# An attention and SwiGLU block on one Trainium2 core: another ScalarE price in the planner, GpSimd work in halves, and a rebuilt end

## The chip, the cores and the metric

The kernel runs on one core of one Trainium2 chip. The core has five engines with instruction queues of their own: TensorE (PE in the profile; its weight loads are PEld), VectorE (DVE), ScalarE (ACT), GpSimd (POOL) and SyncE (SP), which here issues every DMA. They meet through semaphores only. The metric is the device time of one execution in microseconds; lower is better.

## The reference, cut to what matters

One batch of 2048 tokens, model width 512, 32 heads of 16, FFN width 1792, all bf16:

```python
xn  = layernorm(x)
qkv = (xn @ wqkv) -> q, k, v per head          # 32 heads, head size 16
p   = softmax(q @ k.T * 16 ** -0.5)            # 2048 x 2048 per head
att = (p @ v).reshape(2048, 512) @ wo
ffn = (silu(xn @ w1) * (xn @ w3)) @ w2
out = x + att + ffn
```

## The kernel before

**Tiling.** The queries are cut into 4 chunks of 512, the heads into 8 groups of 4; a chunk and a group make a unit, 32 in all. A unit has 64 pairs: one block of 128 keys, two heads of the group, 512 queries. A pair is two score matmuls (L1774) into two neighbouring PSUM banks, then an exponential over 128x1024 elements, then matmuls with V into PSUM bank 7, where a row of ones beside V gathers the softmax's denominator (L2027). There are 2048 score matmuls, so 1024 pairs.

**Two ways to exponentiate.** A pair goes to ScalarE as one activation (L1837, tile PT), or to VectorE as integer arithmetic on bf16 bit patterns: L1909 ("p1") reads the scores from PSUM, and a chain of four instructions over two such pairs, L1951, L1958, L1967 and L1973, makes three bf16 arrays in tile xd whose products with V are summed. So a VectorE pair costs three times the V matmuls of a ScalarE pair. Three PSUM buffers of two banks (0-1, 2-3, 4-5) hold scores; bank 6 takes all dense tiles: projections, FFN, output.

**End of a unit.** VectorE copies bank 7 into U (L2045); DMAs bring the denominators into Lc; VectorE takes reciprocals (L2065); DMAs spread them over the partitions as R. For every second unit GpSimd multiplies U by R into onorm (L2092, 128x512, 15 times; function `e5`). Unit 30's half is multiplied on VectorE (L2086), and unit 31, the last, has a path of its own (`last_end`): ScalarE copies bank 7 (L2107), small fp32 matmuls sum and spread (L2114, L2132), VectorE multiplies (L2140).

**Output tiles.** `tile_OUT(tg, part)` makes 128 tokens of output. Part 3 sums the 14 FFN groups in PSUM, and VectorE adds the residual xr and keeps the result as fp32 in osum (L1599). Part 4 (first three chunks) and part 2 (last chunk) sum the attention groups; VectorE adds osum (L1612) and a DMA of 128 KB stores the tile (L1619). Part 2 of every second tile adds osum in PSUM instead, through an fp32 identity matmul (L1593, tile idf), and ScalarE may copy it out (L1608). A group is four matmuls of 32 output columns each that run side by side.

**Order.** A planner, `_Sched`, writes out the whole order of every engine's queue when the kernel is built. It steps a clock of its own by 0.02 us and hands out work as engines come free, with prices for each instruction (`a_cost` ScalarE, `d_cost` VectorE from PSUM, `s_cost` VectorE from SBUF), a tail until others see a result (`_TAILS`), and gaps between matmuls of one tiling and the other (`_time`). VectorE takes a pair whenever it is about to come free (`try_d`, `d_due`); ScalarE takes the others (`try_a`). On the chip the queues run in that order, each as its semaphores allow. `bg` lists the FFN and output tiles in the order wanted; `dense_banks` and `start_tile` let them in. `left[u]` counts a unit's pairs not yet scored, `st["pos"]` the score matmuls issued. In the last unit VectorE gets no pairs when `left` is at `D_STOP` = 6.

**The very end.** Every engine loads a flag and branches around a slow path that this data doesn't need; then SyncE waits on all 24 DMA semaphores (`emit_end`, L141).

Of the kernel before, what the change touches and what calls it, by code (L numbers as in the profile page):

```python
# [13 lines left out]
_NDMA_SEMS = 24  # L14
# [6 lines left out]
class _Prog:  # L21
# [115 lines left out]
    def emit_end(self, e, handle, dma_sems):  # L137
        if e == "sp":
            for i in range(_NDMA_SEMS):
                if self.dma_final[i] > 0:  # L140
                    handle.wait_ge(dma_sems[i], self.dma_final[i])  # L141


_LAT = 0.06
_LATS = {("pe", "act"): 0.041, ("pe", "dve"): 0.053, ("dve", "pool"): 0.083, ("pool", "dve"): 0.033, ("act", "dve"): 0.033}
_TAILS = {"act": 0.182, "dve": 0.083, "pool": 0.05, "sp": 0.0}


class _Sched(_Prog):
# [25 lines left out]
    def _time(self, op, deps, dur, tail, mode=None, rows=None):  # L175
# [7 lines left out]
        if mode == "row":  # L183
            if lm == "row":
                gap = 0.217 if rows & lr else 0.007
            else:
                gap = 0.318
            start = max(ready, ls + gap)
            self.pem = (mode, rows | lr if gap < 0.1 and start < ls + 0.2 else rows, start)
            self.free["pe"] = start + 0.01  # L190
        elif mode == "col":
            start = max(ready, ls + (0.217 if lm == "col" else 0.318))
            self.pem = (mode, frozenset(), start)
            self.free["pe"] = start + 0.2
        else:
            start = max(ready, ls + (0.217 if lm == "x" else 0.318))
            self.pem = (mode, frozenset(), start + dur - 0.217)
            self.free["pe"] = start + dur
# [838 lines left out]
def _plan_fast(nc, ps, flag, A_x, A_wqkv, A_wo, B_w1, B_w3, B_w2, out):  # L1037
# [30 lines left out]
    NW = 3  # L1068
    PVQ = 28
    A_SOON = 0.7  # L1070
    D_SOON = 0.6
# [15 lines left out]
    with ctx:  # L1087
# [67 lines left out]

        a_cost = lambda n: 0.049 + 0.000834 * n
        d_cost = lambda n: 0.054 + 0.00106 * n
# [364 lines left out]
        def tiles_FFN(sc, fc):  # L1522
# [40 lines left out]
            def cond_g():  # L1563
# [4 lines left out]
                if sc > 0 and not all(("HF", (sc - 1) * 4 + i) in done for i in range(4)):  # L1568
# [3 lines left out]
                    _T("Y%d_%d" % (sc, fc), mk(1), evac_u, cond=lambda: ("G%d_%d" % (sc, fc)) in done)]  # L1572

        ON_B = (NQC * NP) % NON

        def tile_OUT(tg, part):
            qc, ts = divmod(tg, 4)

            def og(g, slot, key):
                return (lambda i: onorm[:, slot, ts * 128 + 32 * i:ts * 128 + 32 * i + 32], wo[:, g, :],  # L1580
                        [("ON", slot), ("wor", g)],
                        lambda: have(key))
            ffn = [(lambda i, fc=fc: hT[:, fc, ts * 128 + 32 * i:ts * 128 + 32 * i + 32], w2[:, fc, :],
                    [("hT", fc), ("w2", fc)], None) for fc in range(FC)]
            ats = [og(g, (qc * NP + g) % NON, ("ON", qc, g)) for g in range(NP)]
            gr = {2: ats + [og(NP - 1, ON_B, ("ON", qc, "B"))], 3: ffn, 4: ats, 0: ffn + ats}[part]
            by_pe = part == 2 and ts % 2 == 1
            groups = []
            for k, (lh, rh, rd, cd) in enumerate(gr):
                groups.append((lambda e, bk, lh=lh, rh=rh, k=k: col_groups(lh, rh, D)(  # L1590
                    e, bk, k == 0, k == len(gr) - 1), rd, cd, DG))
            if by_pe:
                groups.insert(1, (lambda e, bk: e.matmul(bank(bk), idf[:, :], osum[:, ts, :], start=False, stop=False),  # L1593
                                  [("idf",), ("osum", ts)], None, 0.95))

            def evac(bk, o, rel):
                def e1(eng="dve"):
                    if part == 3:
# [6 lines left out]
                        return  # L1605
                    other = osum[:, ts, :] if part in (2, 4) else xr[:, ts % 2, :]
                    if by_pe and eng == "act":
                        fn = lambda e: e.activation(osb[:, ts, :], bank(bk), ACTF.Identity)  # L1608
                    elif by_pe:
                        fn = lambda e: e.tensor_copy(osb[:, ts, :], bank(bk))  # L1610
                    else:
                        fn = lambda e: e.tensor_tensor(osb[:, ts, :], bank(bk), other, ALU.add)  # L1612
                    q = P.op(eng, fn,
                             reads=[("ps", bk), ("osum", ts) if part in (2, 4) else ("xr", ts % 2)],
                             writes=[("osb", ts), ("xn", ts)],
                             dur=d_cost(512) if eng == "dve" else a_cost(512))
                    rel(q)
                    done[("XE", tg)] = q.end
                    P.post("sp", lambda: P.dma(lambda e: e.dma_start(out_v[:, tg, :], osb[:, ts, :]),  # L1619
                                               reads=[("osb", ts)], writes=[("out", tg)], kb=128),  # L1620
                           ready=q.end + _LAT, prio=1)
                if by_pe:
                    P.post2({"dve": lambda: e1("dve"), "act": lambda: e1("act")}, ready=o.end + _LAT,
                            prios={"dve": 2, "act": 1})
                else:
                    P.post("dve", e1, ready=o.end + _LAT, prio=1, cond=lambda: part in (2, 4) or ("xr", tg) in done)

            def cond():
                if part == 4:
                    return have(("OSUM", tg), ("ON", qc, NP - 1))  # L1630
                if part == 2:
                    return have(("OSUM", tg)) and st["pos"] >= NR
                if not have(*[("hT", qc, fc) for fc in range(FC)]):
# [7 lines left out]
            def start():  # L1641
                def load():
                    P.dma(lambda e: e.dma_start(xr[:, ts % 2, :], x_v[:, tg, :]), writes=[("xr", ts % 2)], kb=128)
                    done[("xr", tg)] = P.t
                P.post("sp", load, ready=P.t, prio=1, cond=lambda: tg < 2 or ("XE", tg - 2) in done)
            return _T("O%d_%d" % (tg, part), groups, evac, cond=cond, start=None if part in (2, 4) else start)


        st = {"dbl": 0, "pos": 0, "pv": 0, "dbal": 0, "nd": 0, "lastA": -1.0, "n_exp": 0, "wait_a": 0, "hold_d": 0, "last_par": 0}
        pbuf = [0.0] * 3  # L1650
# [40 lines left out]
        for sc in range(NQC):  # L1691
# [5 lines left out]
            for ts in range(4):  # L1697
                bg.append(tile_OUT(sc * 4 + ts, 3))
        for ts in range(4):
            bg.append(tile_OUT((NQC - 1) * 4 + ts, 2))  # L1700
# [8 lines left out]
        def dense_banks():  # L1709
            if st["pos"] >= NR and st["n_exp"] >= NR:  # L1710
                return [6, 0, 1, 2, 3, 4]
            if st["pos"] == 0:
                return [6, 4, 5, 2, 3]
            if st["early"]:
                return [6, 4, 5]
            return [6]
# [158 lines left out]
        def try_d():  # L1875
# [28 lines left out]
            def p1():  # L1904
                if sl["y"] is None:
                    sl["y"] = free_slot(yfree)
                    yfree[sl["y"]] = 1e9
                ys = sl["y"]
                q = P.op("dve", lambda e: e.tensor_scalar(dsl[:, ys, 1024 * c:1024 * c + 1024], ps[:, b0 * 512:b0 * 512 + 1024],  # L1909
                                                          YB, G_LO, ALU.add, ALU.max),  # L1910
# [128 lines left out]
        def unit_end(u, o):  # L2039
# [33 lines left out]
            def e4():  # L2073
# [4 lines left out]
                if h or u == NU - 2:  # L2078
                    eng = "dve" if u == NU - 2 else "pool"
                    P.post(eng, lambda: e5(eng), ready=q.end + _LAT, prio=0, cond=lambda: u // 2 < NON or all(  # L2080
                        ("OUT", (u // 2 - NON) // NP * 4 + i) in done for i in range(4)))

            def e5(eng):
                on = (u // 2) % NON
                if u == NU - 2:
                    q = P.op(eng, lambda e: e.scalar_tensor_tensor(onorm[:, on, :], U[:, 0, :], msk[:, 0:1], R[:, :],  # L2086
                                                                   ALU.mult, ALU.mult),
                             reads=[("Uc",), ("msk", 0)] + [("R", j_, h_) for j_ in range(4) for h_ in range(2)],
                             writes=[("ON", on)], dur=0.68)
                    done[("ON", qc, pi)] = q.end + _LAT  # L2090
                    return
                q = P.op(eng, lambda e: e.tensor_tensor(onorm[:, on, :], U[:, 0, :], R[:, :], ALU.mult),  # L2092
                         reads=[("Uc",)] + [("Uo", j_) for j_ in range(4)] +
                         [("R", j_, h_) for j_ in range(4) for h_ in range(2)], writes=[("ON", on)],
                         dur=0.6 if eng == "dve" else 1.3)
                done[("ON", qc, pi)] = q.end + _LAT
                done[("e5", u // 2)] = q.end
            if u == NU - 1:
# [3 lines left out]
        def last_end(o):  # L2102
# [36 lines left out]
            def norm_b():  # L2139
                q = P.op("dve", lambda e: e.scalar_tensor_tensor(onorm[:, ON_B, :], U[:, 1, :], msk[:, 1:2], bank(PV),  # L2140
                                                                 ALU.mult, ALU.mult),
                         reads=[("Ut",), ("ps", PV), ("msk", 1)], writes=[("ON", ON_B)], dur=0.597)
                done[("ON", qc, "B")] = q.end + _LAT
# [5 lines left out]
        def start_tile(urgent_only):  # L2149
            banks = [b for b in dense_banks() if bank_free[b] <= P.t and not any(a.bank == b for a in active)]  # L2150
            if not banks or len(active) >= (4 if st["pos"] >= NR or st["pos"] == 0 else 2):
                return
# [30 lines left out]
        def try_dense():  # L2183
            start_tile(False)
            for a in active:
# [6 lines left out]
                if not a.groups:  # L2192
# [5 lines left out]
                    if a.name[0] == "O":  # L2198
                        tg_, pt_ = a.name[1:].split("_")
                        if pt_ != "3":  # L2200
                            done[("OUT", int(tg_))] = o.end
                        if pt_ in "013":
                            done[("HF", int(tg_))] = o.end
# [147 lines left out]
```

## Time and profile before

| | |
|---|---|
| median of 8 runs | 801.57 us (800.11 to 803.56) |
| the profiled execution | 800.48 us, span 798.7 us, mean granted TensorE clock 0.997 |
| busy in the span | PE 754.2, DVE 766.1, ACT 774.9, POOL 33.1 us |
| exponentials on ScalarE (L1837) | 801, 1160 ns each on average |
| pairs on VectorE (L1909) | 223, 1216 ns each |
| VectorE chain L1951, L1958, L1967, L1973 | 112 each; 697, 1232, 681, 709 ns |
| GpSimd multiplications (L2092) | 15, 1508 ns each |
| fp32 identity matmuls (L1593) | 4 instructions, 2.3 us in all |

The span runs from the first to the last instruction; the time has some 2 us around it. In the profile a line such as `L1837 ACT ACTIVATE f_PT<-ps ... x801 | 751.9, 1160 | 4.8 <-PE` gives line, engine, operation, output and inputs, count, busy time in us, mean ns of one, and the engine's idle time before them with what ended it. Instructions of one engine overlap at their ends, so the mean of one is longer than the distance between two. In a timeline a row gives start and length in us, engine, line and count, and in brackets the idle time before it and who ended that.

### The profile page before, as it was taken

How to read it: one execution, taken by the hardware profiler on the slowest of the kernel's cores; microseconds unless marked ns; L12 is line 12 of the kernel's file. 1: busy time of each engine (PE TensorE's matmuls, PEld its weight loads, DVE VectorE, ACT ScalarE, POOL GpSimd, SP SyncE). 2: the span in 40 equal slices, each digit the busy share in tenths (PEclk: the TensorE clock that was granted, in tenths of full speed). 3: DMA queues.
4: the chain of work that ended last, by engine and by line, in shares of the span. 5: the costliest groups of instructions: out<-in, count | busy, mean ns of one | idle time of the engine just before them, and what ended most of it. 6: DMA issues, size and time to landing. Idle time of an engine off the chain costs nothing.

```text
span 798.7 us, 21147 instructions
## 1 busy us (share of the span) xinstructions
PE 754.2 (94%) x9157; PEld 222.6 (28%) x9157; DVE 766.1 (96%) x1032; ACT 774.9 (97%) x876; POOL 33.1 (4%) x45
## 2 busy tenths in 40 slices
PE   8998999999999999999999999999999999999996
PEld 6322322222222222222222222222222222222222
DVE  8898999999999999999999999999999999999984
ACT  6999999999999999999999999999999999999993
POOL 3100100000000000000000000000000000000000
PEclk9999999999999999999999999999999999999998
DMA  7032233332222233133221233322123341232211
GB/s 212 2 62 67 16 42 35 43 46 23 48 37 29 29 46 49 32 46 55 36 21 31 33 48 44 53 28 51 20 22 41 48 55 19 51 34 23 29 8 33
DMA packets 83727, 32.91 MB, mean 41 GB/s; under 512 B 72104, under 2 KB 80040, under 8 KB 83624
## 3 DMA queue, kind: packets, MB, share of 16 engines
q1 hardware_dynamic: 83624, 31.46, 27.4%
q8 instruction: 74, 1.21, 0.6%
q14 instruction: 29, 0.24, 0.1%
HBM read 22.81 MB, written 2.10 MB: 31 GB/s over the span
## 4 chain that ended last, share of the span: by engine, by line
ACT 65%; DVE 18%; PE 14%; issue 1%; DMA 1%; POOL 0%; SPq 0%; DVEq 0%
ACT f_PT L1837 62%; DVE f_xd L1909 5%; PE ps L1328 5%; PE ps L1774 5%; PE ps L2027 4%; DVE f_xd L1958 3%; ACT f_th L1542 3%; DVE f_xd L1951 2%; DVE f_xd L1973 1%; DVE f_xd L1967 1%; DVE f_t L1546 1%; DVE f_hT L1556 1%; DVE f_stats L1252 1%; DMA f_R<-f_Rrow 1%; DVE f_U L2045 0%
## 5 line engine op out<-in xcount | busy, mean ns | idle before, releaser
L1837 ACT ACTIVATE f_PT<-ps 128x1024 bf16<-128x1024 f32 x801 | 751.9, 1160 | 4.8 <-PE ps L1774 2.6
L1774 PE MATMUL ps<-f_QT,f_KT 32*128 32x512 bf16 x2048 | 313.7, 385 | 25.9 <-ACT f_PT L1837 17.5
L1909 DVE TENSOR_SCALAR f_xd<-ps 128x1024 int16<-128x1024 f32 x223 | 271.1, 1216 | 4.9 <-PE ps L1774 3.7
L2027 PE MATMUL ps<-f_PT,f_Vaug 128*17 128x512 bf16 (+1 forms) x1602 | 211.7, 385 | 1.0 <-DVE f_U L2045 0.4
L2027 PE MATMUL ps<-f_xd,f_Vaug 128*17 128x512 bf16 (+1 forms) x1338 | 185.9, 385 | 4.3 <-DVE f_U L2045 1.8
L1774 PEld LDWEIGHTS ps<-f_QT,f_KT 32*128 32x128 bf16 x2048 | 79.1, 91 | 332.6 <-ACT f_PT L1837 272.2
L1328 PE MATMUL ps<-f_xnT,f_w 128*32 128x512 bf16 x1792 | 140.7, 384 | 3.9 <-DVE f_t L1546 3.2
L1958 DVE TENSOR_TENSOR f_xd<-f_xd 128x2048 bf16<-128x2048 bf16 x112 | 138.0, 1232 | 0.0
L1951 DVE TENSOR_SCALAR f_xd<-f_xd 128x2048 int16<-128x2048 int16 x112 | 78.0, 697 | 2.2 <-PE ps L2027 1.6
L1973 DVE TENSOR_SCALAR f_xd<-f_xd 128x2048 int16<-128x2048 int16 x112 | 79.4, 709 | 0.0
L1967 DVE TENSOR_SCALAR f_xd<-f_xd 128x2048 int16<-128x2048 int16 x112 | 76.3, 681 | 0.0
L1328 PE MATMUL ps<-f_w,f_hT 128*32 128x512 bf16 x896 | 75.5, 384 | 0.0
L2027 PEld LDWEIGHTS ps<-f_PT,f_Vaug 128*17 128x17 bf16 (+1 forms) x1602 | 50.9, 92 | 58.6 <-issue 45.7
L2027 PEld LDWEIGHTS ps<-f_xd,f_Vaug 128*17 128x17 bf16 (+1 forms) x1338 | 44.8, 92 | 49.9 <-issue 27.3
L1328 PEld LDWEIGHTS ps<-f_xnT,f_w 128*32 128x32 bf16 x1792 | 36.1, 94 | 62.5 <-issue 52.4
L2092 POOL TENSOR_TENSOR f_onorm<-f_U,f_R 128x512 bf16<-128x512 f32 x15 | 22.6, 1508 | 709.8 <-DMA f_R<-f_Rrow 709.8
L1542 ACT ACTIVATE f_th<-ps 128x512 f32<-128x512 f32 x56 | 41.6, 743 | 0.0
L1546 DVE SCALAR_TENSOR_TENSOR f_t<-f_th,ps 128x512 bf16<-128x512 f32 x56 | 38.0, 679 | 1.8 <-ACT f_th L1542 1.3
L1556 DVE SCALAR_TENSOR_TENSOR f_hT<-f_t,ps 128x512 bf16<-128x512 bf16 x56 | 38.0, 678 | 0.8 <-PE ps L1328 0.6
L1328 PEld LDWEIGHTS ps<-f_w,f_hT 128*32 128x32 bf16 x896 | 17.9, 94 | 25.5 <-issue 21.3
L1328 PE MATMUL ps<-f_wo,f_onorm 128*32 128x512 bf16 x272 | 21.5, 384 | 0.8 <-DVE f_wkv L1599 0.3
L2045 DVE COPY f_U<-ps 128x512 f32<-128x512 f32 x31 | 21.2, 684 | 0.0
(82 smaller groups left out, 239.2 us busy)
## 6 DMA issues: line engine op xcount, KB each, us to landing
f_w<-in_B_w_dram SPq DMA_DIRECT2D x112, 128.0 KB, 2.4
f_R<-f_Rrow SPq DMA_DIRECT2D x124, 32.0 KB, 4.0
f_xr<-in_A_x_dram SPq DMA_DIRECT2D x16, 128.0 KB
out_dram<-f_xn_sb SPq DMA_DIRECT2D x16, 128.0 KB
f_U<-f_U SPq DMA_DIRECT2D x60, 32.0 KB, 2.0
f_w<-in_B_w_dram SPq DMA_DIRECT2D x7, 256.0 KB
f_xd<-in_A_x_dram SPq DMA_DIRECT2D x3, 512.0 KB
f_xd<-in_A_x_dram SPq DMA_DIRECT2D x2, 256.0 KB
```

The costliest lines, as they stand in the source:

```text
L1328: ins = e.matmul(bank(bk)[32 * i:32 * i + 32, 0:ncols], make_lhsT(i), rhs_ap, start=start, stop=stop, tile_position=(0, 32 * i))
L1542: q = P.op("act", lambda e: e.activation(th[:, ss, :], bank(bk), ACTF.Tanh, scale=0.5), reads=[("ps", bk)], writes=[("th", ss)], dur=a_cos ...
L1546: q2 = P.op("dve", lambda e: e.scalar_tensor_tensor(t1[:, ss, :], th[:, ss, :], 1.0, bank(bk), ALU.add, ALU.mult), reads=[("th", ss), ("ps ...
L1556: q = P.op("dve", lambda e: e.scalar_tensor_tensor(hT[:, fc, :], t1[:, ss, :], 0.5, bank(bk), ALU.mult, ALU.mult), reads=[("t1", ss), ("ps ...
L1774: ins = e.matmul(bank(b), l_, r_, start=True, stop=True, tile_position=(rp, 0))
L1837: q = P.op("act", lambda e: e.activation(PT[:, s_, :], ps[:, b0 * 512:(b0 + 2) * 512], ACTF.Exp, scale=ASC, bias=ABIAS), reads=[("ps", b0) ...
L1909: q = P.op("dve", lambda e: e.tensor_scalar(dsl[:, ys, 1024 * c:1024 * c + 1024], ps[:, b0 * 512:b0 * 512 + 1024], YB, G_LO, ALU.add, ALU. ...
L1951: P.op("dve", lambda e: e.tensor_scalar(dsl[:, NY + m_, 0:n], y, 0x7F, 0x3F00, ALU.bitwise_and, ALU.bitwise_or), reads=YK, writes=[("ds", ...
L1958: q_ = P.op("dve", lambda e: e.tensor_tensor(t_ap.bitcast(BF16), y.bitcast(BF16), t_ap.bitcast(BF16), ALU.mult), reads=YK + [("ds", NY + m ...
L1967: q_ = P.op("dve", lambda e: e.tensor_scalar(g_ap, y, -G_LO, 0.0, ALU.add, ALU.max), reads=YK, writes=[("g", g_, k) for k in range(n // 51 ...
L1973: q_ = P.op("dve", lambda e: e.tensor_scalar(y, y, 0x7F80, None, ALU.bitwise_and), reads=YK, writes=YK, dur=s_cost(n), name="e", lock=True)
L2027: ins = e.matmul(bank(PV)[32 * j:32 * j + (17 if g % 2 == 0 else 32), :], v_, p_, start=s0, stop=s1, tile_position=(0, 32 * j))
```

## The change

- The planner's price of a ScalarE instruction goes from 0.049 + 0.000834 n to 0.0615 + 0.000834 n us, its tail from 0.182 to 0.105; three gaps between matmuls change by 0.002 to 0.007.
- The GpSimd multiplication is cut into two of 128x256 (`e5h`). Each is issued in the planner step in which an L1909 is issued, and waits on the VectorE instruction before that L1909. Output tiles read onorm by halves.
- L2086 is posted 2.5 us later in the planner's clock (`R_LAG`).
- The fp32 identity matmuls go. The last chunk's first three tiles take part 3 and part 2 with VectorE's addition; its fourth tile is one sum in PSUM (part 5): 14 FFN groups, the residual through a bf16 identity, the attention groups; ScalarE copies it out.
- `late()`: output tiles of the last chunk may start, and bank 4 may be used for them, when the last unit has at most 6 pairs to be scored, VectorE holds none and buffer 2 is free; before, this came when all scores were issued. The fourth tile waits for `late()`.
- The last chunk's outputs are stored by two DMAs of two tiles each.
- At the end SyncE waits only on the DMAs that it doesn't know to be done from waits before.

```diff
-            for i in range(_NDMA_SEMS):
-                if self.dma_final[i] > 0:
-                    handle.wait_ge(dma_sems[i], self.dma_final[i])
+            left = [op for op in self.ops["sp"] if op.token[1] == self.dma_final[op.token[0][1]]
+                    and self.known.get(op.token[0], 0) < op.token[1]]
+            for op in left:
+                handle.wait_ge(dma_sems[op.token[0][1]], op.token[1])
...
-_TAILS = {"act": 0.182, "dve": 0.083, "pool": 0.05, "sp": 0.0}
+_TAILS = {"act": 0.105, "dve": 0.083, "pool": 0.05, "sp": 0.0}
...
-                gap = 0.318
+                gap = 0.325
...
-            start = max(ready, ls + (0.217 if lm == "col" else 0.318))
+            start = max(ready, ls + (0.219 if lm == "col" else 0.32))
...
+    R_LAG = 2.5
...
-        a_cost = lambda n: 0.049 + 0.000834 * n
+        a_cost = lambda n: 0.0615 + 0.000834 * n
...
+        def late():
+            return left[NU - 1] <= D_STOP and st["hold_d"] == 0 and pbuf[2] <= P.t or st["pos"] >= NR
...
-            gr = {2: ats + [og(NP - 1, ON_B, ("ON", qc, "B"))], 3: ffn, 4: ats, 0: ffn + ats}[part]
-            by_pe = part == 2 and ts % 2 == 1
+            last_b = [og(NP - 1, ON_B, ("ON", qc, "B"))]
+            res = [(lambda i: ident[:, 32 * i:32 * i + 32], xr[:, ts % 2, :], [("ident",), ("xr", ts % 2)],
+                    lambda: have(("xl", tg)))]
+            gr = {2: ats + last_b, 3: ffn, 4: ats, 5: ffn + res + ats + last_b}[part]
...
-            if by_pe:
-                groups.insert(1, (lambda e, bk: e.matmul(bank(bk), idf[:, :], osum[:, ts, :], start=False, stop=False),
-                                  [("idf",), ("osum", ts)], None, 0.95))
...
+                    if part == 5:
+                        q = P.op("act", lambda e: e.activation(osb[:, ts, :], bank(bk), ACTF.Identity),
+                                 reads=[("ps", bk)], writes=[("osb", ts), ("xn", ts)], dur=a_cost(512))
...
+                    fin_o.append(ts)
+                    if len(fin_o) % 2 == 0:
+                        t0, t1 = sorted(fin_o[-2:])
+                        P.post("sp", lambda: P.dma(lambda e: e.dma_start(
+                            out_v[:, 4 * qc + t0:4 * qc + t1 + 1:t1 - t0, :], osb[:, t0:t1 + 1:t1 - t0, :]),
...
-                    return have(("OSUM", tg)) and st["pos"] >= NR
+                    return have(("OSUM", tg)) and (st["pos"] >= NR or late())
+                if part == 5 and tg == NT - 1 and not late():
+                    return False
...
-                bg.append(tile_OUT(sc * 4 + ts, 3))
-        for ts in range(4):
+                bg.append(tile_OUT(sc * 4 + ts, 5 if sc == NQC - 1 and ts > 2 else 3))
+        for ts in range(3):
             bg.append(tile_OUT((NQC - 1) * 4 + ts, 2))
...
-            if st["pos"] >= NR and st["n_exp"] >= NR:
-                return [6, 0, 1, 2, 3, 4]
+            if late():
+                return [6] + [k for k in ((4, 0, 1, 2, 3) if st["pos"] >= NR else (4,)) if pbuf[k // 2] <= P.t]
...
+                st["p1_at"], st["p1_op"] = P.t, P.ops["dve"][-1]
                 q = P.op("dve", lambda e: e.tensor_scalar(dsl[:, ys, 1024 * c:1024 * c + 1024], ps[:, b0 * 512:b0 * 512 + 1024],
...
-                    P.post(eng, lambda: e5(eng), ready=q.end + _LAT, prio=0, cond=lambda: u // 2 < NON or all(
-                        ("OUT", (u // 2 - NON) // NP * 4 + i) in done for i in range(4)))
+                    P.post(eng, (lambda: e5(eng)) if eng == "dve" else (lambda: e5h(0)), ready=q.end + _LAT + (R_LAG if eng == "dve" else 0.0), prio=0, cond=lambda: (eng == "dve" or beside_p1()) and (u // 2 < NON or all(
+                        ("OUT", (u // 2 - NON) // NP * 4 + i) in done for i in range(4))))
+
+            def beside_p1():
+                return st["p1_at"] == P.t
+
+            def e5h(i):
+                on = (u // 2) % NON
+                cs = slice(256 * i, 256 * i + 256)
+                q = P.op("pool", lambda e: e.tensor_tensor(onorm[:, on, cs], U[:, 0, cs], R[:, cs], ALU.mult),
+                         reads=[("Uc",)] + [("Uo", j_) for j_ in range(4)] +
+                         [("R", j_, h_) for j_ in range(4) for h_ in range(2)], writes=[("ON", on, i)], dur=0.72,
+                         extra=[st["p1_op"]])
...
-            if not banks or len(active) >= (4 if st["pos"] >= NR or st["pos"] == 0 else 2):
+            if not banks or len(active) >= (4 if late() or st["pos"] == 0 else 2):
```

## The prediction

> **What bounds the kernel now.** I read the page first: busy shares, the chain, the costliest groups.
>
> ```profile
> PE 754.2 (94%) x9157; PEld 222.6 (28%) x9157; DVE 766.1 (96%) x1032; ACT 774.9 (97%) x876; POOL 33.1 (4%) x45
> ACT 65%; DVE 18%; PE 14%; issue 1%; DMA 1%; POOL 0%; SPq 0%; DVEq 0%
> L1837 ACT ACTIVATE f_PT<-ps 128x1024 bf16<-128x1024 f32 x801 | 751.9, 1160 | 4.8 <-PE ps L1774 2.6
> L1909 DVE TENSOR_SCALAR f_xd<-ps 128x1024 int16<-128x1024 f32 x223 | 271.1, 1216 | 4.9 <-PE ps L1774 3.7
> L2092 POOL TENSOR_TENSOR f_onorm<-f_U,f_R 128x512 bf16<-128x512 f32 x15 | 22.6, 1508 | 709.8 <-DMA f_R<-f_Rrow 709.8
> ```
>
> ScalarE bounds the body: from 32 to 776 us it idles visibly for about 2.5 us. The 1160 ns of one exponential is no pitch, for neighbours overlap: start to start is mostly 904 ns, in the mean 917 (722 neighbouring pairs with no idle shown). Summed over 32 to 776 us, ScalarE's starts lie 14.4 us behind a pitch of 904 ns (477 for the FFN's tanh); that loss is what the body can give. VectorE idles 14.8 us there. Next the timeline, around one GpSimd multiplication:
>
> ```profile
> 466.07 1.31 POOL L2092 TENSOR_TENSOR f_onorm<-f_U,f_R 128x512 bf16<-128x512 f32 x1 [43.98 <-DMA f_R<-f_Rrow]
> 466.16 2.30 DVE L1958 TENSOR_TENSOR f_xd<-f_xd 128x2048 bf16<-128x2048 bf16 x1
> ...
> 468.39 1.21 DVE L1909 TENSOR_SCALAR f_xd<-ps 128x1024 int16<-128x1024 f32 x1
> ...
> 469.66 0.40 PE L1774 MATMUL ps<-f_QT,f_KT 32*128 32x512 bf16 x4 [0.74 <-DVE f_xd L1909]
> ...
> 470.43 1.94 ACT L1837 ACTIVATE f_PT<-ps 128x1024 bf16<-128x1024 f32 x2 [0.62 <-PE ps L2027]
> ```
>
> Read down: beside GpSimd the VectorE multiplication takes 2.30 us where its median is 1.217; L1909 comes late, TensorE stands 0.74 us for its buffer, and ScalarE stands 0.62 us. The stall reached the bound. Third, the last head group, timeline and windows (the windows' columns are stretch, its length, busy time and count of PE, PEld, DVE, ACT and POOL, granted clock, DMA):
>
> ```profile
> 777.28 0.75 DVE L2086 SCALAR_TENSOR_TENSOR f_onorm<-f_U,f_msk,f_R 128x512 bf16<-128x512 f32 x1 [2.01 <-DMA f_R<-f_Rrow]
> ...
> 779.82 0.61 PE L1774 MATMUL ps<-f_QT,f_KT 32*128 32x512 bf16 x2 [0.83 <-DVE f_xd L1909]
> ...
> 781.03 1.02 ACT L1837 ACTIVATE f_PT<-ps 128x1024 bf16<-128x1024 f32 x1 [0.65 <-PE ps L2027]
> ```
> ```profile
> 779.00:780.00 1.00, 0.18 (x2) 0.10 (x2) 1.00 (x2) 1.00 (x2) 0.00 (x0) 0.87 0.00 0
> 780.00:781.00 1.00, 1.00 (x10) 0.17 (x8) 1.00 (x3) 0.38 (x1) 0.00 (x0) 0.50 0.06 16
> ```
>
> VectorE stands 2.01 us before L2086 for a DMA; its chain behind that is late, TensorE runs dry, and its granted clock falls to 0.50 until about 783.1. Last, the end:
>
> ```profile
> 785.40 1.13 PE L1593 MATMUL ps<-f_wkv,f_idf 128*128 128x512 f32 x2
> 785.57 0.60 ACT L2107 ACTIVATE f_U<-ps 128x512 f32<-128x512 f32 x1 [0.74 <-PE ps L2027]
> ...
> 790.30 1.29 DVE L1612 TENSOR_TENSOR f_xn_sb<-ps,f_wkv 128x512 bf16<-128x512 f32 x2 [0.29 <-PE ps L1328]
> ...
> 790.83 1.13 PE L1593 MATMUL ps<-f_wkv,f_idf 128*128 128x512 f32 x2
> ...
> 792.98 0.60 ACT L1608 ACTIVATE f_xn_sb<-ps 128x512 bf16<-128x512 f32 x1 [1.87 <-PE ps L1328]
> 793.60 0.33 SPq L1619 DMA_DIRECT2D out_dram<-f_xn_sb  x1
> ```
> ```profile
> L141 SPq EVENT_SEMAPHORE  x12: 17/28/28, 797.5 to 798.2; - x12
> ```
>
> The second fp32 identity matmul stands between the outputs; behind the last output DMA SyncE walks through 12 wait instructions before the span ends at 798.7.
>
> **The change part by part**, against the profiled execution (800.48 us, span 798.7), negative is a gain.
>
> *GpSimd halves.* Of the 15 multiplications, six (at 228, 322, 421, 466, 516 and 612 us) stretch a VectorE instruction by 0.85 to 1.09 us, three by 0.06 to 0.48, and six only touch L1909 (median 1.218 with or without) or miss. All stretches together are 7.0 us of VectorE. In the 7 us behind those six, ScalarE's starts lose 0.42, 0.65, 0.67, 0.95, 0.89 and 0.64 us, together 4.2; behind the other nine 0.11 each on average. So 4.2 - 6 x 0.11 = 3.5 us reach the bound. After the change a half starts when the VectorE instruction before an L1909 ends, beside that L1909 (pitch 1.13 us). What a half costs, no row shows: between half of the fastest whole, 1.27 / 2 = 0.64, and 1.27. I take a value near the lower end, since the work halves; up to some 1.05 it fits beside L1909. The waits added to GpSimd hold up nothing but its second half: onorm is needed by the next output tiles, and 44 to 52 us lie between two such multiplications. Term **-3.5**, from -5 (small stretches too) to +3.5 (halves that miss L1909 and stretch as before, twice as often). [...]
>
> *The lower ScalarE rate.* It is a price inside the planner (0.049 to 0.0615 per instruction): no instruction gets slower. The 1024-column price goes from 0.903 to 0.9155, between the usual 0.904 and the mean 0.917. Planned ScalarE work grows by 0.0125 x 872 = 10.9 us. The planner hands pairs to VectorE whenever that comes free; with 0.917 us per ScalarE pair and 2.64 us of VectorE per pair (1.133 for L1909, and half of 0.616 + 1.157 + 0.636 + 0.603 for the chain, pitches), (10.9 - d)/0.917 = d/2.64 gives d = 8.1 us and 3 pairs: about 798 and 226. ScalarE loses 2.75 us of work; VectorE gains 7.9, against 14.8 idle plus 7.0 freed. Not all that idle is usable, and a reordered plan may wait elsewhere: **-1.0**, from -6 (scores in time, below) to +4. The changed TensorE and tail prices (0.325, 0.105) act through the order alone and go with this.
>
> *The last head group.* L2086 is posted 2.5 us later, so the chain no longer queues behind its DMA. The four last exponentials start at 779.16, 781.03, 782.41 and 783.80; at 0.904 the last would start at 781.87: 1.9 us. Against that, the last output tile now sums its FFN part late: 14 groups and the residual's, 15 x 0.217 = 3.25 us of TensorE (0.217 us is the pitch of such groups of four matmuls), and saves one addition of 0.68 us on VectorE. Its cover: TensorE is idle for 1.83 us from 776 to 780 (windows 0.73 + 0.80 + 0.46 + 0.18 busy) and loses 3.2 x 0.5 = 1.6 to the half clock, 3.4 in all. It just fits; without cover it costs up to 3.25. **-1.5**, from -1.9 to +1.7. On the clock the row decides: it fell after four microseconds in which TensorE was busy for 2.17. The skill's rule (TensorE: Matmul & The Clock Gate, What's actually happening) asks for an idle window of some 3.4 us; by it the clock would not have fallen here, and filling would save the 1.83 alone.
>
> *The last outputs.* The second identity pair (1.06 us on the chain) goes; of the first, only 786.17 (end of L2107) to 786.52 is on the chain. Then VectorE is late next: three additions in series behind 790.30, 2 x 0.60 + 0.68, end at 792.2 against 793.58 now, while ScalarE copies the fourth tile. **-1.5**, from -0.6 to -1.8. Paired DMAs: the last is issued at the same event; its packets ended at 795.84, the first end wait ran at 797.54, so some 1.7 us cover the other 128 KB.
>
> *End waits.* 797.54 to 798.26 is 0.72 us for 12 instructions; two or so remain: **-0.6**, from -0.3 to -0.7.
>
> Sum: -3.5 - 1.0 - 1.5 - 1.5 - 0.6 = -8.1, so 792.4 for the profiled execution. The median of eight, 801.57, is 1.1 above it: **793.5**.
>
> **Rivals.**
> *Scores stop being late.* Of the 14.4 us, 3.5 are GpSimd's, some 2 a steady 18 ns on 119 exponentials; 8.9 are exponentials waiting for scores by 30 to 700 ns. Truer prices could remove 5 more: 788.5. For it: the waits are on L1774. Against: TensorE is 96% busy.
> *The late tile is not hidden.* If its tile starts only after the last scores, the 3.25 us lie on the end: 796.7. The condition that opens the early start (six pairs left, a buffer free) makes this possible.
> *The body gives nothing.* New order, new waits; only the last three terms, -3.6: 798.0.
> *VectorE becomes the bound (slower).* If its idle time is waiting that no plan can use, only the freed 7.0 us count. Each pair moved costs 2.64; with the end's 3.6 gained, it turns at (7.0 + 3.6)/2.64 = 4 pairs; at 6 it is 15.8 - 10.6 = 5.2 slower, 806.8. Against: the sum gives 3 pairs.
>
> **How the numbers follow.** Forecast 0.42 (own range 790.5 to 796.5), scores in time 0.15, tile not hidden 0.13, body nothing 0.13, no difference 0.06, VectorE bound 0.11. Measurement tells 0.2%, 1.6 us, from no change. The first four are faster: 0.83, same 0.06, slower 0.11. The range 787.5 to 800.5 leaves out the slower case, most of the same, and the tail of the best.
>
> **What would show it.** Right: 796 to 799 exponentials and 225 to 228 of L1909; 30 GpSimd halves near 0.7 us, and no L1951, L1958 or L1973 over 1.6 us; no wait of 2 us before L2086; clock 1.00 to the end; the last output DMA some 8.3 us behind the start of the last exponential (793.60 - 783.80 = 9.8 now); two or three L141. Wrong: over 230 of L1909 with longer ScalarE idle, TensorE waiting on L1909 as often as before, or 15 FFN groups after the last exponential.

## The result, and the profile after

The changed kernel takes 798.12 us (median of 13 runs) against 800.92 us (36 runs) before: a ratio of 0.9962, 95% interval 0.9953 to 0.9971, so 3.0 us faster by the ratio. The forecast was 8.1 us, with 793.5 as the time; the sign is right, the size is not. The time lies at the 798.0 of the rival "the body gives nothing", but not for its reason (see below). The profiled execution took 798.14 us, its span is 796.3. Its page:

```profile
PE 750.8 (94%) x9169; PEld 226.5 (28%) x9169; DVE 768.7 (97%) x1039; ACT 772.6 (97%) x872; POOL 38.1 (5%) x60
L1847 ACT ACTIVATE f_PT<-ps 128x1024 bf16<-128x1024 f32 x798 | 747.7, 1135 | 5.3 <-PE ps L1784 4.3
L1920 DVE TENSOR_SCALAR f_xd<-ps 128x1024 int16<-128x1024 f32 x226 | 275.0, 1217 | 4.1 <-PE ps L1784 3.6
L2100 POOL TENSOR_TENSOR f_onorm<-f_U,f_R 128x256 bf16<-128x256 f32 x30 | 25.2, 844 | 704.1 <-DMA f_R<-f_Rrow 413.8
```

(Lines have moved: L1847, L1784 and L1920 are L1837, L1774 and L1909 of before, L1962, L1969, L1978 and L1984 the chain L1951, L1958, L1967 and L1973, L1330 the dense matmuls L1328.) The counts are those forecast: 798 exponentials and 226 VectorE pairs. What was not forecast stands in the windows (length; busy time and count of PE, PEld, DVE, ACT, POOL; granted clock; DMA) and in the timeline of TensorE's FFN-output groups. First two lines of the kernel before, then the changed kernel:

```profile
767.00:770.00 3.00, 3.00 (x38) 0.92 (x40) 2.90 (x6) 3.00 (x4) 0.00 (x0) 1.00 0.05 9
771.65 0.61 PE L1328 MATMUL ps<-f_w,f_hT 128*32 128x512 bf16 x8
```
```profile
761.00:764.00 3.00, 2.50 (x24) 0.70 (x22) 3.00 (x5) 3.00 (x5) 0.00 (x0) 1.00 0.00 0
767.00:770.00 3.00, 2.08 (x14) 0.50 (x12) 3.00 (x4) 3.00 (x4) 0.00 (x0) 0.83 0.24 14
770.00:773.00 3.00, 3.00 (x22) 0.57 (x20) 2.97 (x5) 2.94 (x4) 0.00 (x0) 0.50 0.95 31
773.00:776.00 3.00, 3.00 (x20) 0.64 (x18) 2.87 (x4) 2.40 (x4) 0.00 (x0) 0.54 0.14 44
```
```profile
756.39 0.39 PE L1330 MATMUL ps<-f_w,f_hT 128*32 128x512 bf16 x4
776.36 0.39 PE L1330 MATMUL ps<-f_w,f_hT 128*32 128x512 bf16 x2
```

Between 756.4 and 776.4 us TensorE has no dense work at all; before, these groups ran on until 771.9. It runs short of work, and from 769.0 its clock is halved for 6.8 us; ScalarE, which had not waited there before, gets 2.40 busy us out of 3. Another 3.4 us at half clock begin at 311.6. The GpSimd halves are no clean gain either:

```profile
563.67 2.06 POOL L2100 TENSOR_TENSOR f_onorm<-f_U,f_R 128x256 bf16<-128x256 f32 x2 [49.34 <-DMA f_R<-f_Rrow]
...
563.92 1.22 DVE L1962 TENSOR_SCALAR f_xd<-f_xd 128x2048 int16<-128x2048 int16 x1
...
565.07 1.21 DVE L1984 TENSOR_SCALAR f_xd<-f_xd 128x2048 int16<-128x2048 int16 x1
```

Both halves stand beside SBUF instructions whose usual length is 0.69 us, and not beside an L1920. Seven VectorE instructions are stretched by 3.4 us in all (nine by 7.0 before). Last, the end, with the end waits:

```profile
787.61 3.42 PE L1330 MATMUL ps<-f_wo,f_onorm 128*32 128x512 bf16 x60
...
790.01 0.69 DVE L1614 TENSOR_TENSOR f_xn_sb<-ps,f_wkv 128x512 bf16<-128x512 f32 x1 [0.17 <-PE ps L1330]
791.09 0.69 DVE L1614 TENSOR_TENSOR f_xn_sb<-ps,f_wkv 128x512 bf16<-128x512 f32 x1 [0.39 <-PE ps L1330]
```
```profile
L142 SPq EVENT_SEMAPHORE  x3: 28/28/28, 795.7 to 795.9; - x3
```

When the last normalisation starts (787.65), TensorE still has 15 groups (60 matmuls) to go, not four, and VectorE's additions wait for it. The last exponential ends 1.5 us sooner than before (783.30 against 784.83), the last copy out 1.8 us sooner (791.78 against 793.58). Three wait instructions are left of twelve.

### The profile page after: what moved, and what is told of

Its sections match the earlier page's. It is cut to its first block, busy times and chain, and to the rows that moved or that the text cites. A ratio compares the mean times of both kernels' runs of the same rounds, so it can differ in the third digit from the quotient of the medians.

```text
span 796.3 us, 21182 instructions
## 1 busy us (share of the span) xinstructions
PE 750.8 (94%) x9169; PEld 226.5 (28%) x9169; DVE 768.7 (97%) x1039; ACT 772.6 (97%) x872; POOL 38.1 (5%) x60
## 4 chain that ended last, share of the span: by engine, by line
ACT 59%; DVE 24%; PE 13%; issue 1%; DMA 1%; POOL 0%; SPq 0%; DVEq 0%
ACT f_PT L1847 56%; DVE f_xd L1920 8%; PE ps L1330 5%; PE ps L1784 4%; DVE f_xd L1969 4%; PE ps L2038 3%; DVE f_xd L1962 2%; ACT f_th L1544 2%; DVE f_xd L1978 2%; DVE f_xd L1984 2%; DVE f_hT L1558 2%; DVE f_t L1548 1%; DMA f_xd<-in_A_x_dram 1%; DVE f_U L2056 1%; DVE f_stats L1254 1%
## 5 line engine op out<-in xcount | busy, mean ns | idle before, releaser
L1847 ACT ACTIVATE f_PT<-ps 128x1024 bf16<-128x1024 f32 x798 | 747.7, 1135 | 5.3 <-PE ps L1784 4.3
L1784 PE MATMUL ps<-f_QT,f_KT 32*128 32x512 bf16 x2048 | 311.1, 387 | 26.1 <-ACT f_PT L1847 20.6
L1920 DVE TENSOR_SCALAR f_xd<-ps 128x1024 int16<-128x1024 f32 x226 | 275.0, 1217 | 4.1 <-PE ps L1784 3.6
L2038 PE MATMUL ps<-f_xd,f_Vaug 128*32 128x512 bf16 (+1 forms) x1356 | 182.7, 386 | 3.9 <-DVE f_xd L1969 1.6
L1784 PEld LDWEIGHTS ps<-f_QT,f_KT 32*128 32x128 bf16 x2048 | 79.6, 91 | 323.1 <-ACT f_PT L1847 260.3
L1330 PE MATMUL ps<-f_xnT,f_w 128*32 128x512 bf16 x1792 | 140.6, 386 | 3.0 <-DVE f_t L1548 1.2
L1969 DVE TENSOR_TENSOR f_xd<-f_xd 128x2048 bf16<-128x2048 bf16 x113 | 137.2, 1214 | 0.0
L1962 DVE TENSOR_SCALAR f_xd<-f_xd 128x2048 int16<-128x2048 int16 x113 | 80.5, 712 | 2.7 <-PE ps L2038 1.9
L1984 DVE TENSOR_SCALAR f_xd<-f_xd 128x2048 int16<-128x2048 int16 x113 | 77.9, 690 | 0.0
L1978 DVE TENSOR_SCALAR f_xd<-f_xd 128x2048 int16<-128x2048 int16 x113 | 77.4, 685 | 0.0
L1330 PE MATMUL ps<-f_w,f_hT 128*32 128x512 bf16 x896 | 72.9, 383 | 0.2
L2038 PEld LDWEIGHTS ps<-f_xd,f_Vaug 128*32 128x32 bf16 (+1 forms) x1356 | 44.6, 92 | 51.3 <-issue 27.6
L2100 POOL TENSOR_TENSOR f_onorm<-f_U,f_R 128x256 bf16<-128x256 f32 x30 | 25.2, 844 | 704.1 <-DMA f_R<-f_Rrow 413.8
L1330 PEld LDWEIGHTS ps<-f_xnT,f_w 128*32 128x32 bf16 x1792 | 36.8, 94 | 62.6 <-issue 52.0
L1330 PEld LDWEIGHTS ps<-f_w,f_hT 128*32 128x32 bf16 x896 | 19.3, 95 | 23.7 <-issue 16.3
L1330 PE MATMUL ps<-f_wo,f_onorm 128*32 128x512 bf16 x272 | 19.9, 382 | 0.2 <-DVE f_QT L1458 0.2
```

Source lines behind the costliest of these rows:

```text
L1330: ins = e.matmul(bank(bk)[32 * i:32 * i + 32, 0:ncols], make_lhsT(i), rhs_ap, start=start, stop=stop, tile_position=(0, 32 * i))
L1784: ins = e.matmul(bank(b), l_, r_, start=True, stop=True, tile_position=(rp, 0))
L1847: q = P.op("act", lambda e: e.activation(PT[:, s_, :], ps[:, b0 * 512:(b0 + 2) * 512], ACTF.Exp, scale=ASC, bias=ABIAS), reads=[("ps", b0) ...
L1962: P.op("dve", lambda e: e.tensor_scalar(dsl[:, NY + m_, 0:n], y, 0x7F, 0x3F00, ALU.bitwise_and, ALU.bitwise_or), reads=YK, writes=[("ds", ...
L1969: q_ = P.op("dve", lambda e: e.tensor_tensor(t_ap.bitcast(BF16), y.bitcast(BF16), t_ap.bitcast(BF16), ALU.mult), reads=YK + [("ds", NY + m ...
L1978: q_ = P.op("dve", lambda e: e.tensor_scalar(g_ap, y, -G_LO, 0.0, ALU.add, ALU.max), reads=YK, writes=[("g", g_, k) for k in range(n // 51 ...
```

## The experiments

Theory A: TensorE runs dry (short of work) in the last unit because the planner has used up the dense work and holds the last tile back, and the half clock that follows gives back some 3 us. Theory B: the halves often miss their L1920, because R lands later than planned. Theory C: VectorE, with three pairs more, is the bound. All runs were timed beside the kernel before, whose median was 801.4 to 801.9 us; ratios are to it, with 95% intervals.

### e1: the tile not held

```diff
-                if part == 5 and tg == NT - 1 and not late():
-                    return False
```

> The changed kernel without the rule that holds the last output tile back until late(): its 14 FFN groups may run as soon as the FFN is done. Theory A (TensorE runs dry at 762 to 769 us because that tile is held, and its clock halves for 6.8 us): FFN groups again between 762 and 770, no half clock there in the profile, 1 to 2 us faster than the changed kernel (about 796.5). Theory B (the GpSimd halves that miss their L1909 eat the gain): no change, 798. Theory C (VectorE, with 3 more pairs, is the bound): no change, 798.

797.71 us, 0.9954 (0.9941 to 0.9966): not told from the changed kernel. The edit did not do what was meant: another condition of the same tile waits for unit 30's onorm, so its groups still ran from 774.9 us on, and the profile shows 10.2 us of half clock from 766.7. It says nothing for or against A.

### e2: all end waits

```diff
-            left = [op for op in self.ops["sp"] if ...]
-            for op in left:
-                handle.wait_ge(dma_sems[op.token[0][1]], op.token[1])
+            for i in range(_NDMA_SEMS):
+                if self.dma_final[i] > 0:
+                    handle.wait_ge(dma_sems[i], self.dma_final[i])
```

> The changed kernel with all 24 end waits, nothing else; the order of every queue stays. All theories: 0.6 us slower than the changed kernel (798.7), 12 wait instructions of L141 and a distance from the last output DMA to the end of 5.1 us as before; if something other than SyncE's waits ends the span, no difference.

798.51 us, 0.9964 (0.9951 to 0.9977): the time can't tell half a microsecond. The traces can: from the first of the end waits to the end of the span it is 1.1 us here (794.97 to 796.11) and 0.6 in the changed kernel (795.73 to 796.34), with 12 and 3 wait instructions.

### e3: the halves later

```diff
-ready=q.end + _LAT + (R_LAG if eng == "dve" else 0.0)
+ready=q.end + _LAT + R_LAG
```

> The changed kernel with the first GpSimd half posted 2.5 us later in the planner's clock, so that its R has landed when its L1909 comes; the other queues keep their order. Theory B (13 of 30 halves miss their L1909 because R lands later than planned, 3.4 us of stretched VectorE): at most 3 halves beside L1951 or L1984, stretches under 1 us, 1 to 2 us faster (796.5). Theory A: stretches gone but at most 0.5 us faster, as the half clock stays. Theory C: as B, since VectorE gains 3 us.

796.36 us, 0.9938 (0.9925 to 0.9950): 1.9 us by the ratios, with the order of every queue unchanged; only what the halves wait on differs. What the halves waited for, by line, first in the changed kernel, then here (columns: ns min/median/max; us, times):

```profile
L2100 POOL TENSOR_TENSOR f_onorm<-f_U,f_R x30: 721/730/2118, 82.0 to 759.7; 128x256 bf16<-128x256 f32 x30
...
  DMA f_R<-f_Rrow: 413.8, 9
```
```profile
L2100 POOL TENSOR_TENSOR f_onorm<-f_U,f_R x30: 723/728/734, 82.9 to 757.6; 128x256 bf16<-128x256 f32 x30
...
  DMA f_R<-f_Rrow: 83.8, 2
```

Nine first halves had been released by the landing of R and not by VectorE; now two are, no half is longer than 0.734 us, and no instruction of the chain is stretched. ScalarE's starts between 32 and 760 us lose 11.9 us against 15.6. The changed kernel's profile holds the half clock at 311.6 in this stretch; e1, e2 and e10, which have the same order there and no half clock, lose 13.9, 14.5 and 13.4. B holds, for about 2 us. The half clock is longer here than in any other run (13.7 us from 761 us), so A is still open.

### e4: the multiplication whole

```diff
-onorm[:, on, cs], U[:, 0, cs], R[:, cs]   (twice, each beside an L1909)
+onorm[:, on, :], U[:, 0, :], R[:, :]      (once, when R has landed)
```

> The changed kernel with the GpSimd multiplication whole again and free to start when R lands, as in the kernel before (15 of 128x512). The planner's order shifts a little. If the halves gave what was forecast: 15 multiplications, some 7 us of stretched VectorE, 2 to 3.5 us slower than the changed kernel (800 to 801.5). If they gave only half, as the remaining stretches of 3.4 us say: 1 to 2 us slower (799.5). If the stretches don't reach ScalarE any more: 798.

799.51 us, 0.9971 (0.9963 to 0.9980): 0.7 us by the ratios, with intervals that overlap. But the edit changes more than the halves. From some 425 us on the planner's order is another one, the dense work comes later (third tile's FFN groups until 772.6 us, 756.4 in the changed kernel), and the stretch in which the changed kernel has its half clock is full:

```profile
770.00:773.00 3.00, 3.00 (x36) 0.75 (x34) 2.93 (x5) 3.00 (x5) 0.00 (x0) 1.00 0.05 8
```

So the 0.7 us are what the halves gave less what the half clock took, and this run does not isolate the halves. Against e3, which has the half clock, e4 is 2.6 us slower; against e10 below, which hasn't, 4.2.

### e5: useless matmuls in the empty stretch

```diff
+            if NR - 200 < st["pos"] < NR and P.free["pe"] <= P.t and P.t >= P.pem[2] + 0.34 and idle((6,)):
+                # four matmuls of ones by xnT into bank 6, side by side, results unread
```

> As the run with the later GpSimd half (796.4 against 801.6 before), plus 13 groups of four matmuls into the free PSUM bank 6, with results that nobody reads, wherever the planner leaves TensorE without work in the last 200 score matmuls. Theory A (TensorE runs dry, its clock halves for 13.7 us from 761 us in that run and ScalarE waits): no half clock between 755 and 776 us, last exponential 1.5 to 2.5 us sooner, 794 to 795 in all, though 2.8 us of useless matmuls were added. Rival D (the half clock is harmless, since ScalarE and not TensorE is the bound there): 796.4 or a little more.

793.03 us, 0.9898 (0.9883 to 0.9913): 3.2 us faster than e3 by the ratios, which differs by 13 groups of matmuls that compute nothing used, and by a few neighbours in the last unit's order that change places for them. The windows:

```profile
767.00:770.00 3.00, 2.80 (x32) 0.72 (x29) 2.72 (x4) 3.00 (x5) 0.00 (x0) 1.00 0.66 62
770.00:773.00 3.00, 3.00 (x50) 0.89 (x42) 3.00 (x5) 3.00 (x5) 0.00 (x0) 1.00 0.02 5
773.00:776.00 3.00, 3.00 (x40) 0.85 (x36) 2.15 (x3) 3.00 (x4) 0.00 (x0) 1.00 0.00 0
```

The clock stays at 1.00, ScalarE is busy throughout, and the last exponential ends at 778.44 us (781.13 in e3). ScalarE's loss up to 760 us hardly differs (11.9 us in e3, 12.3 here): 2.7 of the 3.2 us have arisen by the end of the last exponential, in the stretch that was empty. A holds; D falls.

### e6: real work in the empty stretch

```diff
-                if not have(("w13", idx)):
+                if not have(("w13", idx)) or st["pos"] < 33.6 * idx:
...
-                if part == 5 and tg == NT - 1 and not late():
-                    return False
-                if not have(*[("hT", qc, fc) for fc in range(FC)]):
+                if not have(*[("hT", qc, fc) for fc in range(FC)]) or qc == NQC - 1 and st["pos"] < 1890 + 36 * ts:
...
-                return have(("ON", qc, NP - 1))
+                return True
```

> As the run with the later GpSimd half, with real work in place of the empty one: the last output tile may start as soon as its FFN inputs are there (its attention groups wait for their own inputs only), and the start of the last FFN and FFN-output tiles is spread over the score position (33.6 per FFN block, then 36 per tile). Theory A: FFN groups between 755 and 776 us, full clock there, 794 to 795; and the end 0.5 us shorter, since the FFN groups no longer stand behind the last exponential. Rival D: 796.

792.79 us, 0.9894 (0.9879 to 0.9909), clock 1.00 until the last exponential. The last FFN group runs at 764.8 us, and the end has the form that the prediction drew:

```profile
783.51 1.05 PE L1330 MATMUL ps<-f_wo,f_onorm 128*32 128x512 bf16 x16 [0.76 <-DVE f_fm L2234]
...
784.18 1.89 DVE L1614 TENSOR_TENSOR f_xn_sb<-ps,f_wkv 128x512 bf16<-128x512 f32 x3 [0.49 <-PE ps L1330]
```

Four groups behind the normalisation and three additions in one piece: 7.1 us from the last exponential's end to the last copy out (8.5 in the changed kernel, 8.75 before). This version beats both kernels, by 8.5 us against before.

### e7: the prices alone

```diff
-        a_cost = lambda n: 0.049 + 0.000834 * n      # on the kernel before; tail and gaps too
+        a_cost = lambda n: 0.0615 + 0.000834 * n
```

> The kernel before with the four price changes alone (ScalarE 0.0615 and tail 0.105, matmul gaps 0.325, 0.32 and 0.219); the GpSimd multiplication whole, the end as before. Forecast term: 1 us faster than before, 799 exponentials. Theory A: the lower ScalarE rate by itself leaves TensorE idler in the body, more half-clock time than before, so between 1 us faster and 1 us slower (800 to 802).

802.04 us, 1.0009 (0.9998 to 1.0020): no gain, at most 0.2 us by its interval.

### e8: the new end undone

Prices, halves, `R_LAG` and the few end waits as changed; `tile_OUT`, `dense_banks` and the output DMAs as before.

> The changed kernel with the output tiles of before: prices, halves, the later L2086 and the fewer end waits stay; late(), the sum in one bank and the paired DMAs go, the fp32 identity matmuls come back. Forecast terms: 1.5 us for the outputs, so 1.5 slower than the changed kernel (799.6). Theory A with a late tile that cost what it gave: within 0.7 us of the changed kernel (797.5 to 799).

799.10 us, 0.9977 (0.9965 to 0.9988): 1.2 us behind the changed kernel, with overlapping intervals. The expectation left the range between both theories open, and the result falls into it.

### e9: L2086 later, alone

```diff
-P.post(eng, lambda: e5(eng), ready=q.end + _LAT, prio=0
+P.post(eng, lambda: e5(eng), ready=q.end + _LAT + (2.5 if eng == "dve" else 0.0), prio=0
```

> The kernel before with the one edit that posts L2086 2.5 us later: on VectorE's queue L1951, L1973 and L1909 pass it, no other queue changes. Forecast term (last head group, without the moved tile): no idle of 2 us before L2086, clock 1.00 in the last 20 us before the last exponential, last exponential up to 1.9 us sooner, 799.5 to 800.5 (1 to 2 us faster than before). Rival: TensorE runs dry there all the same, since no dense work is left, and the half clock stays: 801.4.

800.53 us, 0.9981 (0.9969 to 0.9992): 1.5 us faster than before. In its profile, taken of an execution of 798.35 us:

```profile
777.39 0.74 DVE L2086 SCALAR_TENSOR_TENSOR f_onorm<-f_U,f_msk,f_R 128x512 bf16<-128x512 f32 x1
779.00:782.00 3.00, 2.11 (x40) 0.72 (x32) 3.00 (x6) 3.00 (x5) 0.00 (x0) 1.00 0.02 5
```

No wait stands before L2086 any more, the clock is 1.00 up to the last exponential, and that ends at 782.99 us, 1.84 sooner than in the profile of before, where the prediction had 1.9.

### e10: the changed kernel, filled

The edit of e5 on the changed kernel.

> The changed kernel with the 13 useless groups of matmuls in the last 200 score matmuls, nothing else. Theory A (the half clock behind 762 us costs the changed kernel as much as it cost the run with the later half, 3.3 us there): 795 to 796. The half clock at 312 us can stay, in some executions. If the clock mattered less before the GpSimd stretches went: 797.

795.35 us, 0.9918 (0.9906 to 0.9931): 3.5 us by the ratios. The clock in the stretch is full:

```profile
770.00:773.00 3.00, 3.00 (x42) 0.77 (x41) 3.00 (x5) 3.00 (x5) 0.00 (x0) 1.00 0.45 55
```

So the empty stretch cost the changed kernel 3.5 us.

### e11 and e12: the old and a middle rate in the paced version (e6)

```diff
-        a_cost = lambda n: 0.0615 + 0.000834 * n
+        a_cost = lambda n: 0.049 + 0.000834 * n      # e12: 0.055
```

> The paced version (792.8) with ScalarE's price back at 0.049 (tail and gaps as changed): some 800 exponentials. Forecast term: 1 us slower than the paced version. If the lower rate only makes the planner run out of dense work sooner, as the 0.7 us loss of the prices alone says: the same or up to 2 us faster. If the order that fits ScalarE's true pitch keeps scores in time (ScalarE lost 11.9 us to late scores in the paced version): 2 to 5 us slower.

> The paced version with ScalarE's price halfway, 0.055. If the price acts through one trend, between the paced version (792.8) and the run with 0.049; if new orders scatter more than the price's trend, outside of these two.

800.78 us, 0.9985 (0.9976 to 0.9994), and 795.98 us, 0.9925 (0.9907 to 0.9943), against 792.79 and 0.9894: 7.3 and 2.5 us by the ratios. The rate is worth far more than 1 us once GpSimd and the clock are out of the way.

### e13: the rate undone in the changed kernel

The edit of e11 on the changed kernel.

> The changed kernel with ScalarE's price back at 0.049, all else as changed: the lower rate undone alone. Forecast term: 1 us slower than the changed kernel (799). If the lower rate carries most of the gain, as the paced runs say (8 us there): 801 or more. If it costs here what it cost alone on the kernel before (0.7 us): 797.4.

801.84 us, 1.0009 (0.9997 to 1.0020): with the old rate the rest of the change gains nothing. The end of its profile:

```profile
786.25 2.56 PE L1330 MATMUL ps<-f_w,f_hT 128*32 128x512 bf16 x44
...
788.85 4.49 PE L1330 MATMUL ps<-f_wo,f_onorm 128*32 128x512 bf16 x80
...
793.39 0.69 DVE L1614 TENSOR_TENSOR f_xn_sb<-ps,f_wkv 128x512 bf16<-128x512 f32 x1 [0.39 <-PE ps L1330]
```

Behind the last exponential, which ends at 782.28, 18 FFN groups start (the last eleven in one piece), and then 20 attention groups: 11.8 us from there to the last copy out, against 8.5. That is the rival "the late tile is not hidden", come true under the old rate. In this profile the last unit has no half clock, since dense work fills it; against e10, whose profile has none there either, the old rate costs 7.3 us.

### e14, e15 and e16: trend or scatter

The paced version with 0.0605 and 0.064 for 0.0615 (e14, e15), and with the old tail and gaps (e16).

> The paced version (792.8) with the price at 0.0605 instead of 0.0615, a change of 1 ns in 916 that no instruction feels but that orders the queues anew. If the price acts as a trend (8 us over 0.0125, so 0.6 us over 0.001): 793.4. If a new order by itself scatters: off by 1.5 us or more, either way.

> The paced version with the price at 0.064, above the mean pitch of 917 ns. Trend: 791.2. If the best price lies where it meets the pitch: 793 to 795. Scatter: off both by more than 1.5 us.

> The paced version with the old tail (0.182) and the old matmul gaps (0.318, 0.217), ScalarE's price at 0.0615. If the ScalarE rate alone carries the price term: within 1 us of 792.8. If the truer gaps and tail carry it: 796 or more.

792.63 us, 0.9891 (0.9875 to 0.9907); 793.74 us, 0.9905 (0.9889 to 0.9921); 794.96 us, 0.9919 (0.9902 to 0.9937). A new order by itself moves the time by 0.2 us in one case and 0.9 in the other, so e11's 7.3 us are more than scatter; e12's 2.5, with an interval that touches that of e6, may not be. The prices from 0.0605 to 0.064 (0.9145 to 0.918 us for 1024 columns, about the mean pitch of 917 ns) are not told apart, and none above was run. With the old tail and gaps it is 2.0 us slower, and the intervals of e6 and e16 overlap, so their worth is not shown.

## Why the prediction was wrong, point by point

**The clock, the step that failed most.** The prediction put the held tile's 3.25 us where they went, found 3.4 us of cover there, and expected "clock 1.00 to the end". It never asked what the tile left behind. The last unit was without dense work for 20 us, TensorE ran short of work, and its clock fell. Shown by e5 and e10: filling the stretch is worth 3.2 and 3.5 us, where the term had 0. Where the output tiles of before are kept (e8), the fourth tile's FFN groups run from 756.0 to 764.6 us:

```profile
764.58 0.40 PE L1329 MATMUL ps<-f_w,f_hT 128*32 128x512 bf16 x4
```

In the changed kernel they come at 776.4. So the held tile left some 9 us empty. The point from which they are empty, the end of the third tile's FFN groups, moves with every order: 760.8 us before, 756.4 as changed, 771.7 with the prices alone (e7), 772.6 with the multiplication whole (e4), 783.2 under the old rate (e13). It is not the price alone that brings it forward; what does stays open. That L2086's stall was the cause in the kernel before was right (e9).

**The GpSimd halves, mis-sized.** The term was -3.5. The sentence that failed is "a half starts when the VectorE instruction before an L1909 ends": that wait is only the earliest time. R must have landed too, and for nine first halves it landed later than the planner thought; this cost 1.9 us (e3). What the halves gave as changed is not isolated: undoing them costs 0.7 us in an order that has no half clock in the last unit (e4), and 4.2 us if e4 is set against e10, which has none there either. A half's length, taken near the lower end between 0.64 and 1.27 us, is 0.73; the two fastest halves, 0.72 us each, take 0.17 us longer than the fastest whole, 1.27.

**The lower rate, mis-sized.** The 3 pairs came out exactly, but the term of -1.0 did not. Undone in the changed kernel the rate costs 3.8 us (e13), or 7.3 where neither profile has a half clock in the last unit (e13 against e10), in the paced version 7.3 (e11); alone on the kernel before the new prices give nothing (e7). In e13 the loss against the changed kernel lies behind the last exponential, where dense work has been left over. On these kernels the rate decides where the dense work ends: the third tile's FFN groups end at 783.2 under the old rate and 756.4 under the new, in the paced version at 782.5 and 753.0. On the kernel before it is the other way round: the last FFN group runs at 771.9, with the new prices at 782.6 (e7). So the direction holds for one order and is no rule; the prediction had taken the rate for a shift of work between two engines alone. Why e11 loses 7.3 us was settled in part: by the profiles its end is 4.7 us longer than e6's (11.8 against 7.1), as in e13, and its last exponential comes 2.7 us later. Two exponentials more (800 against 798) are 1.8 us of that at the mean pitch; the rest stays open.

**L2086.** -1.5, with the moved tile, and -1.5 measured alone (e9). **The last outputs.** -1.5 forecast; 1.2 measured (e8, with the end's other edits), with intervals that overlap and a half clock of 3.4 us in e8 against 6.8, so this term is not isolated. The form of the end was right only once TensorE had no FFN groups left (e6). **End waits.** -0.6, and 0.5 by the traces (e2). **VectorE as the bound** did not come: e5 runs the same 226 pairs and is 8.2 us faster than before.

The two failed steps close the gap one after the other: as changed the kernel gains 3.0 us, with the halves later 5.0 (e3), with the stretch filled as well 8.2 (e5), where the forecast was 8.1. That this meets the forecast so closely is partly luck, since the rate was not right by itself. Luck, too, is how near the rival "the body gives nothing" came: the halves and the rate did gain, and the clock, which that rival left out, took it back. The parts are not to be summed: the prices gain nothing alone (e7), and the rest gains nothing without the rate (e13). Left out of all forecasts was where the dense work would end.

## What to carry to other kernels

Of a tile that is moved, price the place that it leaves as well as the place that it goes to: here a filler of 2.8 us, which kept TensorE's clock up, gained 3.2 to 3.5 us although ScalarE was the bound. In a planned order a price is not only a cost but also a place; look for where background work ends against where the bound engine ends, and pace it so that it lasts to there and no longer. A wait that is to align two engines aligns them only if every other input is there first.

## What the runs showed of the hardware

TensorE's half clock comes in steps: 3.4, 6.8, 10.2 and 13.7 us in the last 40 us of the profiles of before, the changed kernel, e1 and e3, while TensorE still had work. It fell after stretches in which TensorE was still busy for half to two thirds of the time, and not after full idleness: 1.68 of the last 3.41 us in the kernel before (up to 779.73), 2.29 of 3.41 in the changed kernel (up to 768.96). Such a stretch did not always bring a fall: the kernel before passed 3.41 us with 2.09 busy (up to 383.79) at full clock, and e9 3 us with 2.11. It is not the same in every execution: over the changed kernel's 15 runs the mean granted clock went from 0.996 to 0.986 and the time from 796.3 to 800.5 us. The difference of 0.010 is 8.0 us of lost full-speed time (0.010 x 797), for 4.2 us of run time: about half of what TensorE lost reached the end, although ScalarE was the bound. The Trainium skill (TensorE: Matmul & The Clock Gate, What's actually happening) asks for an idle window of some 3.4 us; here, as in the kernel before, the measurement decides: a window that was a third empty was followed by a fall.
